# Cosine phases made by an integer addition on Pool instead of an absolute value on ScalarE, and half of the kernel scalings moved from VectorE to ScalarE

## The chip, the cores and the metric

The kernel runs on one core of one Trainium2 chip. Its time is the device time of one execution in microseconds (us). The core has five engines that run side by side: TensorE (PE in the profile, with its weight loads as PEld), VectorE (DVE), ScalarE (ACT), GpSimd or Pool (POOL) and SyncE (SP, which issues most DMAs). Each engine takes its instructions strictly in order and waits on semaphores for the others.

## The reference

The reference is one transformer-like block with two halves; the second half needs the whole output of the first.

```python
h = layernorm(x) * (1 + ca) + sa                  # x: 1 x 2048 x 640
K = einsum("dn,dnl,dn->dl", C, exp(dt*A * l), dt*B).real   # l = 0..2047, N = 128 complex states
y = irfft(rfft(h, 4096) * rfft(K, 4096))[:2048] + h * Dskip   # one convolution for each of 640 channels
x = x + ga * y
h = layernorm(x) * (1 + cb) + sb
x = x + gb * ((silu(h @ w1) * (h @ w3)) @ w2)     # 640 -> 1728 -> 640
```

The six vectors sa, ca, ga, sb, cb, gb come from `silu(c) @ w_mod`. Everything is float32. What matters here is K: for every channel and state a complex power exp(dt*A*l) is wanted at 2048 positions. The kernel writes l = 64a + b and makes small tables of cosine and sine over a (32 slow values) and b (64 fast values, made as two halves), and lets TensorE multiply and sum over the states.

## The kernel before, in words

The 640 channels are cut into 40 table steps of 16 channels. Work on one step s, by the two-letter words that the program uses for it:

- PH (function `phases`, on Pool, for two steps at once): the angle of each of 32 channels and 64 table places as a 32-bit integer, where 2^32 is a full turn and the addition wraps. Three Pool instructions: a product of `thi` and `iota` (128x1376), an addition of `phi` (128x256), an addition of the parts (128x768). They write one of three buffers `ph`.
- AB and CO (`absph`, `cosine`, on ScalarE, two steps at once): the absolute value of the angle into one of two buffers `cs` (128x2048), then in place the sine of a quarter turn less that value, which is the cosine.
- SI (`sine`, ScalarE, in place in `ph`).
- PA, XA, PQ, XQ: exponents on TensorE and exponentials on ScalarE, into a table `A`.
- E1, E2, A1, A2 (`real1` to `imag2`, VectorE, one step each): the tables times the cosine into `E`, and times the sine in place in `A`. E1 and A1 are 128x1024, E2 and A2 128x512. All four read both their inputs from SBUF. The last reader of a `cs` buffer is E2 of the second step of its pair; the last reader of a `ph` buffer is A2 of that step.
- kg (TensorE) sums over the states into the PSUM tile `pk`; K (`k1evac`, VectorE) adds the skip term to 128x4 of it and writes `pk` times the gate `gaT` into `K1` (128x256); pt (TensorE) and uk (a copy on ScalarE) are the first stage of K's transform.

Beside these steps runs the convolution itself, one group of four frequencies at a time: st (TensorE, tile `p`), kc (a ScalarE copy out of `p`), T (two VectorE products that read `p` in PSUM), Y (two VectorE sums that read one input in PSUM), iv (TensorE, `pz`) and zt (ScalarE copy and store).

Steps 0 to 9 or so are made in a front part in which a table of words orders everything, beside the first layer norm. The rest follows the table `ROUND`, four steps in a round; a word `E1+5` in round r means E1 of step 4r+5. It is an order for each engine's queue: nothing is rearranged at run time.

```python
ROUND = (
    "E1+2 pt+0 CO+4 kg+1 A1+2 kc+2 SI+4 T+2 PA+4 uk+0 XA+4 Y+2 E2+2 st+3 K+1 zt+1 kc+3 A2+2 kg+2 "
    "PQ+4 XQ+4 pt+1 E1+3 uk+1 PA+5 PH+6 XA+5 E2+3 K+2 pt+2 A1+3 E1+4 A2+3 T+3 PQ+5 uk+2 Y+3 XQ+5 "
    "iv+2 PA+6 A1+4 kg+3 XA+6 AB+6 PQ+6 XQ+6 st+4 PA+7 K+3 iv+3 kc+4 XA+7 E1+5 PQ+7 zt+3 T+4 LS+4 "
    "Y+4 XQ+7 SI+6 E2+4 LP+4 A2+4 st+5 kc+5 CO+6 E2+5 PH+8 LC+4 A1+5 LO+4 kg+4 A2+5 pt+3 T+5 uk+3 "
    "iv+4 K+4 Y+5 st+6 iv+5 AB+8 "
).split()
```

LS, LP, LC and LO are small pieces for the second half's modulation, in rounds 2 to 6 alone. After the rounds the convolution drains, and from about 375 us on the second half runs, almost all of it matrix products.

Nearly all instructions are issued through one helper, so that the profile shows line 115 for them; they are told apart by engine and tile.

Of the kernel before, what the change touches and what calls it, by code (L numbers as in the profile page):

```python
# [9 lines left out]
F32 = mybir.dt.float32  # L10
F32R = mybir.dt.float32r
I32 = mybir.dt.int32
AF = mybir.ActivationFunctionType
OP = mybir.AluOpType
# [3 lines left out]
P = 128  # L18
# [3 lines left out]
NA, NB = 32, 64  # L22
DC = 128
NDC = D // DC
SD = 16
# [7 lines left out]
NPH = 2 * NA  # L33
NG = NA // 8
NPG = NPH + NG - 1
LATE = 5
IDLE = 16
TURN = 4294967296.0
# [3 lines left out]
def consts():  # L42

    a = np.arange(NA)[:, None]
    f1 = np.arange(NA)[None, :]
    ang = 2 * np.pi * a * (f1 + 0.25) / NA
    s1 = np.zeros((4, NA, 2, 4, NA))
    s1r = np.zeros((4, NA, 2, NA))
    for q in range(4):
        s1[q, :, 0, q, :] = np.cos(ang)  # L50
        s1[q, :, 1, q, :] = -np.sin(ang)
        s1r[q, :, 0] = np.cos(ang)
        s1r[q, :, 1] = -np.sin(ang)
    s1r = s1r.transpose(0, 1, 3, 2).reshape(P, 2 * NA)
    b = np.arange(NB)[:, None, None]
    g1 = np.arange(NA)[None, :, None]
    f2 = np.arange(NB)[None, None, :]
    th = 2 * np.pi * (b * (g1 + 0.25) / L + b * f2 / NB)
    s2 = np.zeros((2, NB, NA, 2, NB))
    s2[0, :, :, 0] = np.cos(th)  # L60
    s2[1, :, :, 0] = np.sin(th)
    s2[0, :, :, 1] = -np.sin(th)
    s2[1, :, :, 1] = np.cos(th)
    s2 = s2.reshape(P, NA, P)

    i1 = (s2.transpose(2, 1, 0) / L).reshape(2, NB, NA // 2, 2, P).transpose(3, 1, 2, 0, 4).reshape(P, NA // 2, 2, P)
    i1 = i1.reshape(P, NA // 2, 2, 2, 4, 4, 4).transpose(0, 1, 2, 5, 4, 6, 3).reshape(P, NA // 2, 2, P)
    i2 = np.concatenate([np.cos(ang).T, -np.sin(ang).T] * 2)
    f_late = np.arange(4 * LATE, NA)
    i2late = np.stack([i2[f_late], i2[NA + f_late]])  # L70
    i2b = np.einsum("lm,cfa->lcfma", np.eye(4), i2late).reshape(8, 8 - LATE, 4 * P)

    slow = np.roll(np.arange(NA), -8)
    s1 = s1[:, slow].reshape(P, 2, P)

    iota = np.concatenate([-(128 * slow[-8:] + 63), 2 * np.arange(NA) + 1, -1024 * np.arange(1, NG)])
    iota = np.tile(iota.astype(np.int32), (P, 1))

    row = np.arange(P)
    selx = row[:, None] % 8 == np.arange(8)  # L80
    of_m = row[:, None] // 8 % 2 == 1
    stepx = np.where(of_m, np.repeat((0, 0.5), (NB, NA)), np.concatenate([np.arange(NB), 64.0 * slow]))
    is_lo = (row // 16 % 2)[:, None]

    c1 = s1r.reshape(4, NA, 2 * NA).sum(axis=1, keepdims=True).repeat(NA, axis=1).reshape(P, 2 * NA)

    one4 = (np.arange(P) % NA == 0).astype(np.float32)[:, None]

    toq = np.arange(P)[:, None] % 4 == np.arange(P)[None] // NA
    tog = np.arange(P)[:, None] // 4 == np.arange(NA)[None]  # L90
    c1c = np.tile(c1[0], 2)[:, None]
    misc = np.concatenate([selx, stepx, s1r, c1, one4, toq, tog, is_lo, 1 - 2 * is_lo, c1c], axis=1)
    f = lambda v: np.ascontiguousarray(v, dtype=np.float32)
    return {"s1": f(s1), "s2": f(s2), "i1": f(i1), "i2": f(i2), "i2b": f(i2b), "iota": iota, "misc": f(misc),
            "ident": np.eye(P, dtype=np.float32)}


def bc(ap, axis, n):
    v = ap.unsqueeze(axis)
    shape = list(v.shape)  # L100
    shape[axis] = n
    return v.broadcast_to(shape)
# [18 lines left out]
def tile_kernel(ctx: ExitStack, tc: tile.TileContext, a):  # L121
    nc = tc.nc
    V, S, G, PE = nc.vector, nc.scalar, nc.gpsimd, nc.tensor
# [19 lines left out]
    V, S, G, PE, Q = (InOrder(tc, e, (front,)) for e in (nc.vector, nc.scalar, nc.gpsimd, nc.tensor, nc.sync))  # L143

    def keep(ins):

        return tc.keep_in_program_order(ins) if in_order[0] else ins

    def act(*args, **kw):

        return tc.keep_in_program_order(S.activation(*args, **kw))
# [18 lines left out]
    ssm = ExitStack()  # L170
    kp = ssm.enter_context(tc.tile_pool(name="kp", bufs=1, side="right"))
    s1 = kp.tile([P, 2, P], F32, name="s1")
    iota = kp.tile([P, NPG - NA + 8], I32, name="iota")
    gaT = kp.tile([P, D // 4], F32, name="gaT")
    dz = kp.tile([P, D // 4], F32, name="dz")
    V.memset(dz, 0.0)
# [6 lines left out]
    def phase_tile():  # L183
        return php.tile([P, 2 * SD, NPG], I32, name="ph")
# [5 lines left out]
    tp = tabs.enter_context(tc.tile_pool(name="tp", bufs=2, reuse_waits="tile"))  # L190
    once = lambda shape, dt, name: tp.tile(shape, dt, name=name, bufs=1)
    thi = once([P, D], I32, "thi")
# [360 lines left out]
    ph, cs, AA, EC, PK, K1 = {}, {}, {}, {}, {}, {}  # L553
# [40 lines left out]
    def phases(s):  # L594
        sl = slice(s * SD, s * SD + 2 * SD)
        p = phase_tile()
        hold = tc.keep_in_program_order if 0 < s < 4 else keep
        b0 = NA - 8
        base = p[:, :, b0:NA]
        hold(G.tensor_tensor(p[:, :, b0:], bc(thi[:, sl], 2, NPG - b0), bc(iota, 1, 2 * SD), op=OP.mult))  # L600
        keep(G.tensor_tensor(base, base, bc(phi[:, sl], 2, 8), op=OP.add))
        keep(G.tensor_tensor(p[:, :, :b0].rearrange("p k (g j) -> p k g j", j=8), bc(base, 2, NG - 1),
                             bc(p[:, :, NPH:], 3, 8), op=OP.add))
        ph[s] = p[:, :, :NPH]

    def absph(s):
        cs[s] = tp.tile([P, 2 * SD, NPH], F32, name="cs")
        act(cs[s], ph[s], AF.Abs)

    def cosine(s):  # L610
        c = cs.pop(s)
        act(c, c, AF.Sin, scale=-2 * math.pi / TURN, bias=math.pi / 2)
        cs[s], cs[s + 1] = c[:, :SD], c[:, SD:]

    def sine(s):
# [5 lines left out]
    def trig(s):  # L621
        cosine(s)
        sine(s)
# [33 lines left out]
    def k1evac(s):  # L657
        dst = tp.tile([P, SD // 4, NB], F32, name="K1")
        pk = PK.pop(s)
        keep(V.tensor_tensor(pk[:, :, 0], pk[:, :, 0], dz[:, s * 4:s * 4 + 4], op=OP.add))  # L660
        keep(V.tensor_tensor(dst, pk, bc(gaT[:, s * 4:s * 4 + 4], 2, NB), op=OP.mult))
        K1[s] = dst

    PT = {}
# [243 lines left out]
    def conv_part(fn):  # L908
        return lambda k: fn((k - LAG) // 8, (k - LAG) % 8)

    parts = {"PH": phases, "AB": absph, "CO": cosine, "SI": sine, "PA": lambda k: exp_fast((k,)), "XA": fast,
             "PQ": lambda k: exp_slow((k,)), "XQ": slow, "E1": real1, "E2": real2, "A1": imag1, "A2": imag2,
             "kg": kgen, "K": k1evac, "pt": k_stage1, "uk": k_out}
    conv = {"st": conv_part(stage2), "kc": conv_part(k_copy), "T": conv_part(products), "Y": conv_part(sums),
            "iv": conv_part(inverse1), "zt": conv_part(z_store)}
# [86 lines left out]
    for word in FRONT:  # L1002
        name, k = word[:2].rstrip("+"), int(word[len(word[:2].rstrip("+")):])
# [25 lines left out]
    for rnd in range(NS // EB):  # L1029
        if 2 <= rnd < 7:  # L1030
            late_load(rnd - 2)
        for word in ROUND:
            name, k = word[:2].rstrip("+-"), EB * rnd + int(word[len(word[:2].rstrip("+-")):])
# [16 lines left out]
    for tk in range(NS + 1, LAG + 8 * NDC + 2):  # L1050
# [17 lines left out]
        i = tk - 1 - LAG - 8 * NDC + 8  # L1068
# [40 lines left out]
    V, S, G, PE = (InOrder(tc, e, (in_order,)) for e in (nc.vector, nc.scalar, nc.gpsimd, nc.tensor))  # L1109
# [521 lines left out]
def arrange(inputs):  # L1631
    global _CONST
    if _CONST is None:
        _CONST = consts()
    A = np.ascontiguousarray
    g = {k: np.asarray(v) for k, v in inputs.items()}
    x = g["A_u"].reshape(NA, NB, D).transpose(1, 0, 2).reshape(L, D)
    w1, w3 = g["B_w1"], g["B_w3"]
    nf = NFT - 1

    def ftile(w):
        n = w.shape[1] // P
        return w.reshape(KD, P, n, P).transpose(2, 1, 0, 3)

    mixed = np.concatenate([w1[:, nf * P:], w3[:, nf * P:]], axis=1)
    r = {
        "x": A(x),
        "prm": A(np.stack([g[k].T for k in ("A_A_re", "A_A_im", "A_B_re", "A_B_im", "A_C_re", "A_C_im")])),
        "log_dt": A(g["A_log_dt"].reshape(1, D)),
        "D": A(g["A_Dskip"].reshape(1, D)),  # L1650
        "c": A(g["c"].reshape(KD, P).T),
        "w_mod": A(g["w_mod"].reshape(KD, P, 8, 480).transpose(2, 1, 0, 3)),
        "wg": A(np.concatenate([ftile(w1[:, :nf * P]), ftile(mixed)])),
        "wu": A(ftile(w3[:, :nf * P])),
        "w2": A(g["B_w2"]),
    }
    r.update(_CONST)
    return r
# [17 lines left out]
```

## Time and profile before

| | |
|---|---|
| median of 3 runs | 929.85 us (928.87 to 930.47) |
| the profiled execution's own time | 937.06 us |
| span of its trace | 935.1 us |
| busy share of the span | PE 93%, DVE 75%, ACT 58%, POOL 29% |
| the chain that ended last | PE 73%, DVE 9%, ACT 8%, DMA 5% |

The shares are means over stages that differ: the front part (to about 125 us), the rounds (to about 310 us), the drain, and the second half. Rows of the timeline view read: start, duration, engine, line, operation, output<-inputs with partitions x elements, count of merged instructions, and in brackets the idle time of the engine just before and what ended it. Durations of neighbours on VectorE and ScalarE overlap by about 0.1 us (the end of one is still being written when the next begins), so an instruction's share of its engine is the distance to the next start.

### The profile page before, as it was taken

How to read it: one execution, taken by the hardware profiler on the slowest of the kernel's cores; microseconds unless marked ns; L12 is line 12 of the kernel's file. 1: busy time of each engine (PE TensorE's matmuls, PEld its weight loads, DVE VectorE, ACT ScalarE, POOL GpSimd, SP SyncE). 2: the span in 40 equal slices, each digit the busy share in tenths (PEclk: the TensorE clock that was granted, in tenths of full speed). 3: DMA queues.
4: the chain of work that ended last, by engine and by line, in shares of the span. 5: the costliest groups of instructions: out<-in, count | busy, mean ns of one | idle time of the engine just before them, and what ended most of it. 6: DMA issues, size and time to landing. Idle time of an engine off the chain costs nothing.

```text
span 935.1 us, 20139 instructions
## 1 busy us (share of the span) xinstructions
PE 873.9 (93%) x8082; PEld 668.0 (71%) x8082; DVE 700.7 (75%) x1209; ACT 542.0 (58%) x747; POOL 273.8 (29%) x285
## 2 busy tenths in 40 slices
PE   3898879999998899999999999899999999999997
PEld 2545456666666576688888887678888888888886
DVE  5899889999999968677666666577976666654674
ACT  6989889999999632574333333475634333323332
POOL 3333435543544222304222203210332222100341
PEclk9967789999999999999999999999999999999999
DMA  8664375766666967943222239846321312123352
GB/s 264 218 215 172 149 212 169 223 176 190 177 214 183 297 211 223 299 136 99 56 57 57 57 105 242 231 127 197 99 62 52 113 57 57 57 87 97 102 196 82
DMA packets 103328, 140.68 MB, mean 150 GB/s; under 512 B 19940, under 2 KB 62436, under 8 KB 103236
## 3 DMA queue, kind: packets, MB, share of 16 engines
q1 hardware_dynamic: 92532, 113.71, 40.8%
q10 hardware_dynamic: 8272, 18.16, 6.6%
q0 software_dynamic: 2432, 7.54, 2.6%
q8 instruction: 63, 1.03, 0.5%
q14 instruction: 29, 0.24, 0.1%
HBM read 107.92 MB, written 31.46 MB: 149 GB/s over the span
## 4 chain that ended last, share of the span: by engine, by line
PE 73%; DVE 9%; ACT 8%; DMA 5%; issue 3%; POOL 0%; SPq 0%; DVEq 0%; ACTq 0%; POOLq 0%
PE ps L115 54%; PE p L115 6%; PE pz L115 3%; PE pt L115 2%; PE pk L115 2%; DMA rw<-in_w_dram 2%; PE pa L115 2%; PE pu L115 2%; ACT A L115 1%; DVE A L115 1%; DVE uk L115 1%; DVE E L115 1%; ACT cs L115 1%; DVE u L115 1%; ACT uk L115 1%
## 5 line engine op out<-in xcount | busy, mean ns | idle before, releaser
L115 DVE TENSOR_TENSOR s<-ps,s 128x512 f32<-128x512 f32 x138 | 94.8, 687 | 82.6 <-PE ps L115 82.3
L115 ACT CAST gh<-rw 128x640 fp32r<-128x640 f32 x87 | 63.3, 727 | 119.6 <-PE ps L115 90.6
L115 DVE TENSOR_TENSOR gl<-rw,gh 128x640 fp32r<-128x640 f32 x87 | 78.3, 900 | 64.4 <-ACT gh L115 64.4
L115 POOL TENSOR_TENSOR S<-rw 128x256 f32<-128x256 f32 x46 | 36.5, 795 | 233.5 <-DVE S0l L115 155.5
L115 PE MATMUL ps<-xA,gh 128*128 128x512 f32 x280 | 88.0, 392 | 0.6 <-ACT xA L115 0.6
L115 PE MATMUL ps<-gh,uh 128*128 128x512 f32 x224 | 87.7, 392 | 0.0
L115 PE MATMUL ps<-gl,uh 128*128 128x512 f32 x224 | 87.3, 390 | 0.0
L115 POOL TENSOR_TENSOR ph<-thi,iota 128x1376 int32<-128x1376 int32 x20 | 51.2, 2562 | 118.4 <-DVE A L115 103.5
L115 PE MATMUL p<-uk,s 128*64 128x256 f32 x576 | 71.6, 391 | 15.2 <-issue 3.8
L115 DVE TENSOR_TENSOR E<-A,cs 128x1024 f32<-128x1024 f32 (+1 forms) x80 | 80.8, 1021 | 1.6 <-PE pk L115 1.4
L115 PE MATMUL ps<-gh,ul 128*128 128x512 f32 x208 | 81.1, 390 | 0.0
L115 ACT ACTIVATE A<-pa 128x1024 f32<-128x1024 f32 (+1 forms) x80 | 64.3, 815 | 9.9 <-PE pa L115 9.6
L115 PEld LDWEIGHTS p<-uk,s 128*64 128x64 f32 x576 | 41.3, 138 | 36.8 <-DVE Y L115 5.6
L115 PEld LDWEIGHTS ps<-xA,gh 128*128 128x128 f32 x280 | 52.3, 188 | 13.6 <-ACT xA L115 1.2
L115 DVE TENSOR_TENSOR A<-A,ph 128x1024 f32<-128x1024 f32 x40 | 54.1, 1356 | 0.8
L115 PE MATMUL ps<-xA,gl 128*128 128x512 f32 x140 | 54.5, 390 | 0.0
L115 PE MATMUL pt<-s,K 128*64 128x128 f32 x640 | 45.1, 285 | 6.1 <-ACT uk L115 5.9
L115 PEld LDWEIGHTS ps<-gh,uh 128*128 128x128 f32 x224 | 42.2, 188 | 9.4 <-DVE h L115 0.6
L115 ACT ACTIVATE s<-ps 128x512 f32<-128x512 f32 (+1 forms) x33 | 19.7, 597 | 50.0 <-PE ps L115 50.0
L115 PEld LDWEIGHTS ps<-gl,uh 128*128 128x128 f32 x224 | 42.2, 188 | 8.9
L115 PEld LDWEIGHTS pt<-s,K 128*64 128x64 f32 x640 | 35.7, 140 | 14.4 <-ACT uk L115 9.7
L115 POOL TENSOR_TENSOR rw<-rw,gbr 128x512 f32<-128x512 f32 x14 | 20.3, 1453 | 86.6 <-DMA rw<-in_w_dram 84.6
(224 smaller groups left out, 2227.9 us busy)
## 6 DMA issues: line engine op xcount, KB each, us to landing
rw<-in_w_dram ACTq DMA_DIRECT2D x44, 320.0 KB, 3.1
us<-u SPq DMA_DIRECT2D x16, 640.0 KB, 3.5
rw<-in_wg_dram SPq DMA_DIRECT2D x31, 320.0 KB, 2.9
s<-in_s_dram SPq DMA_DIRECT2D x36, 256.0 KB, 4.0
i<-in_i_dram SPq DMA_DIRECT2D x36, 256.0 KB, 4.2
rw<-in_wu_dram SPq DMA_DIRECT2D x28, 320.0 KB, 3.0
uk<-us SPq DMA_DIRECT2D x16, 512.0 KB, 5.9
zs<-zt SPq DMA_DIRECT2D x16, 512.0 KB, 4.3
```

Of the source, the lines that this page charges most:

```text
L115: ins = fn(*args, **kw)
```

## The change

For steps 12 to 39 the cosine is now the sine of the angle plus a quarter turn. The addition is an integer one on Pool (a constant 2^30 from one more column of `iota`, wrapping), from `ph` into `cs`; ScalarE's absolute value is gone there, and the sine takes integers as it did in SI. Besides, for even steps from 12 on, the scaling of `pk` by the gate is made by ScalarE in four 128x64 instructions, each with its gate column as the scale, and no more by VectorE in one 128x256 instruction.

```diff
-    iota = np.concatenate([-(128 * slow[-8:] + 63), 2 * np.arange(NA) + 1, -1024 * np.arange(1, NG)])
+    iota = np.concatenate([-(128 * slow[-8:] + 63), 2 * np.arange(NA) + 1, -1024 * np.arange(1, NG), [1 << 30]])
...
+    quarter = iota[:, NPG - NA + 8:]
...
     def absph(s):
-        cs[s] = tp.tile([P, 2 * SD, NPH], F32, name="cs")
-        act(cs[s], ph[s], AF.Abs)
+        c = tp.tile([P, 2 * SD, NPH], F32, name="cs")
+        if s < 12:
+            act(c, ph[s], AF.Abs)
+            cs[s] = c
+        else:
+            cs[s] = c.bitcast(I32)
+            keep(G.tensor_tensor(cs[s], ph[s], bc(quarter.broadcast_to([P, NPH]), 1, 2 * SD), op=OP.add))
 
     def cosine(s):
         c = cs.pop(s)
-        act(c, c, AF.Sin, scale=-2 * math.pi / TURN, bias=math.pi / 2)
+        if s < 12:
+            act(c, c, AF.Sin, scale=-2 * math.pi / TURN, bias=math.pi / 2)
+        else:
+            i, c = c, c.bitcast(F32)
+            act(c, i, AF.Sin, scale=2 * math.pi / TURN)
         cs[s], cs[s + 1] = c[:, :SD], c[:, SD:]
...
         keep(V.tensor_tensor(pk[:, :, 0], pk[:, :, 0], dz[:, s * 4:s * 4 + 4], op=OP.add))
-        keep(V.tensor_tensor(dst, pk, bc(gaT[:, s * 4:s * 4 + 4], 2, NB), op=OP.mult))
+        if s < 12 or s % 2:
+            keep(V.tensor_tensor(dst, pk, bc(gaT[:, s * 4:s * 4 + 4], 2, NB), op=OP.mult))
+        else:
+            for g in range(SD // 4):
+                act(dst[:, g], pk[:, g], AF.Identity, scale=gaT[:, s * 4 + g:s * 4 + g + 1])
```

Where the instructions stand now is seen on two engines. First Pool's queue in the rounds, before; the numbers behind names tell buffers apart, and each three rows are one PH:

```order
L115 TENSOR_TENSOR ph_1894<-thi_95,iota_75 128x32x43 [waits DVE_49,Activation_49]
L115 TENSOR_TENSOR ph_1894<-ph_1894,phi_96 128x32x8 [waits Pool_49]
L115 TENSOR_TENSOR ph_1894<-ph_1894 128x32x24 [waits Pool_49]
L115 TENSOR_TENSOR ph_2057<-thi_95,iota_75 128x32x43 [waits DVE_49,Activation_49]
L115 TENSOR_TENSOR ph_2057<-ph_2057,phi_96 128x32x8 [waits Pool_49]
L115 TENSOR_TENSOR ph_2057<-ph_2057 128x32x24 [waits Pool_49]
```

So far Pool did nothing here but one PH after the other. The same place of Pool's queue now:

```order
L115 TENSOR_TENSOR cs_1984<-ph_1897,iota_75 128x2048 [waits DVE_49,Activation_49,Pool_49]
L115 TENSOR_TENSOR ph_2063<-thi_95,iota_75 128x32x43 [waits DVE_49]
L115 TENSOR_TENSOR ph_2063<-ph_2063,phi_96 128x32x8 [waits Pool_49]
L115 TENSOR_TENSOR ph_2063<-ph_2063 128x32x24 [waits Pool_49]
L115 TENSOR_TENSOR cs_2160<-ph_2063,iota_75 128x2048 [waits DVE_49,Activation_49,Pool_49]
```

One 128x2048 addition now stands between any two PH, and each waits for VectorE, whose E2 frees the `cs` buffer that is to be written.

Second, VectorE's queue in the middle of a round (E1 and E2 of step 15, K, A1 of step 15, E1 of step 16), before:

```order
L115 TENSOR_TENSOR E_1888<-A_1617,cs_1584 128x16x64
L115 TENSOR_TENSOR E_1888<-A_1617,cs_1584 128x16x32
L115 TENSOR_TENSOR pk_1842<-pk_1842,dz_77 128x4 [waits DVE_49,PE_49]
L115 TENSOR_TENSOR K1_1901<-pk_1842,gaT_76 128x256 [waits DVE_49]
L115 TENSOR_TENSOR A_1617<-A_1617,ph_1502 128x16x64
L115 TENSOR_TENSOR E_1914<-A_1815,cs_1755 128x16x64 [waits Activation_49]
```

The fourth row is the scaling of an even step's `pk`. The same place now:

```order
L115 TENSOR_TENSOR E_1891<-A_1617,cs_1584 128x16x64
L115 TENSOR_TENSOR E_1891<-A_1617,cs_1584 128x16x32
L115 TENSOR_TENSOR pk_1845<-pk_1845,dz_77 128x4 [waits DVE_49,PE_49]
L115 TENSOR_TENSOR A_1617<-A_1617,ph_1502 128x16x64 [waits DVE_49]
L115 TENSOR_TENSOR E_1920<-A_1818,cs_1758 128x16x64 [waits Activation_49]
L115 SCALAR_TENSOR_TENSOR A_1617<-ph_1502,A_1617 128x16x32 [waits DVE_49]
```

The row that wrote `K1` is gone from here; the rest keeps its order. The second row (E2) is the one for which Pool's addition into `cs_1984` waits.

More of the change, by code (lines that the diff above doesn't have):

```diff
@@ L172, in tile_kernel @@
     s1 = kp.tile([P, 2, P], F32, name="s1")
-    iota = kp.tile([P, NPG - NA + 8], I32, name="iota")
+    iota = kp.tile([P, NPG - NA + 9], I32, name="iota")
+    quarter = iota[:, NPG - NA + 8:]
     gaT = kp.tile([P, D // 4], F32, name="gaT")
@@ L599, in phases @@
         base = p[:, :, b0:NA]
-        hold(G.tensor_tensor(p[:, :, b0:], bc(thi[:, sl], 2, NPG - b0), bc(iota, 1, 2 * SD), op=OP.mult))
+        hold(G.tensor_tensor(p[:, :, b0:], bc(thi[:, sl], 2, NPG - b0), bc(iota[:, :NPG - b0], 1, 2 * SD), op=OP.mult))
         keep(G.tensor_tensor(base, base, bc(phi[:, sl], 2, 8), op=OP.add))
```

## The prediction

> **What bounds the kernel now.** The change touches only the rounds, so I read the table of busy times by stretch first, cut at E1+2 (the first VectorE word of a round). Columns: stretch, its length, then busy time of PE, PEld, DVE, ACT, POOL, granted clock, DMA share.
>
> ```profile
> core 0: us, PE busy (x) PEld busy (x) DVE busy (x) ACT busy (x) POOL busy (x), PEclk, DMA share, GB/s
> 208.06:235.48 27.42, 25.50 (x480) 17.92 (x480) 25.84 (x44) 25.97 (x27) 13.02 (x7) 1.00 0.68 197
> sum 135.42, PE 125.25 PEld 89.62 DVE 127.90 ACT 128.14 POOL 65.39; mean PE 25.05 PEld 17.92 DVE 25.58 ACT 25.63 POOL 13.08
> ```
>
> The sum is over five rounds: 135.42 / 5 = 27.08 us a round, in which PE, DVE and ACT are each busy for 25 to 26 us and POOL for 13. Three engines are balanced, and POOL looks half empty. Busy times don't say whose work has slack, so the timeline of VectorE in one round is next. The names of the words stand in the text behind it.
>
> ```profile
> 208.06 1.29 DVE L115 TENSOR_TENSOR E<-A,cs 128x1024 f32<-128x1024 f32 x1
> ...
> 212.03 0.69 DVE L115 TENSOR_TENSOR T<-p,kc 128x512 f32<-128x512 f32 x1 [1.10 <-ACT kc L115]
> ...
> 215.90 1.82 DVE L115 TENSOR_TENSOR E<-A,cs 128x1024 f32<-128x1024 f32 x2
> 217.63 0.16 DVE L115 TENSOR_TENSOR pk<-pk,dz 128x4 f32<-128x4 f32 x1
> 217.83 0.42 DVE L115 TENSOR_TENSOR K<-pk,gaT 128x256 f32<-128x256 f32 x1
> 218.17 1.22 DVE L115 TENSOR_TENSOR A<-A,ph 128x1024 f32<-128x1024 f32 x1
> 219.30 1.22 DVE L115 TENSOR_TENSOR E<-A,cs 128x1024 f32<-128x1024 f32 x1
> 220.44 0.69 DVE L115 SCALAR_TENSOR_TENSOR A<-ph,A 128x512 f32<-128x512 f32 x1
> 221.04 0.68 DVE L115 TENSOR_TENSOR T<-p,kc 128x512 f32<-128x512 f32 x1
> ...
> 223.16 1.69 DVE L115 TENSOR_TENSOR A<-A,ph 128x1024 f32<-128x1024 f32 x1
> ...
> 230.23 0.68 DVE L115 TENSOR_TENSOR E<-A,cs 128x512 f32<-128x512 f32 x1
> 230.83 1.22 DVE L115 TENSOR_TENSOR A<-A,ph 128x1024 f32<-128x1024 f32 x1
> 231.97 0.15 DVE L115 COPY modT<-pm 128x1 f32<-128x1 f32 x1
> ...
> 232.36 0.68 DVE L115 SCALAR_TENSOR_TENSOR A<-ph,A 128x512 f32<-128x512 f32 x1
> ```
>
> VectorE runs without a gap except for T+2 (212.03), which waits 1.10 us for ScalarE's kc. So VectorE sets the round, with ScalarE close behind. One row is too long: A1+4 at 223.16 takes 1.69 us, its like at 218.17 takes 1.22. Pool's timeline tells why.
>
> ```profile
> 221.26 2.50 POOL L115 TENSOR_TENSOR ph<-thi,iota 128x1376 int32<-128x1376 int32 x1 [8.87 <-DVE A L115]
> 223.85 1.50 POOL L115 TENSOR_TENSOR ph<-ph,phi 128x256 int32<-128x256 int32 x1
> ...
> 233.19 2.51 POOL L115 TENSOR_TENSOR ph<-thi,iota 128x1376 int32<-128x1376 int32 x1 [5.21 <-DVE A L115]
> ```
>
> Pool's product ends at 223.76. If A1+4 could not start before that, it ends near 223.76 + 1.1 = 224.86; the row ends at 224.85. (The small addition behind it, at 223.85, is long in its turn; more on it below.) Two collisions from the front part, a DVE and a POOL row each, show the same more grossly:
>
> ```profile
> 26.82 2.51 POOL L115 TENSOR_TENSOR ph<-thi,iota 128x1376 int32<-128x1376 int32 x1
> 27.21 3.19 DVE L115 TENSOR_TENSOR E<-A,cs 128x1024 f32<-128x1024 f32 x1 [0.21 <-ACT cs L115]
> ...
> 97.49 1.22 DVE L115 TENSOR_TENSOR E<-A,cs 128x1024 f32<-128x1024 f32 x1
> 97.71 3.35 POOL L115 TENSOR_TENSOR ph<-thi,iota 128x1376 int32<-128x1376 int32 x1 [4.61 <-DVE A L115]
> ```
>
> At 27.21 Pool is first: E takes 3.19 us and ends at 30.40, which is Pool's end (29.33) plus 1.07. At 97.71 VectorE is first: Pool takes 3.35 us instead of 2.50 and ends at 101.06, that is 98.56 plus 2.50. **Pool's arithmetic and the E and A words, both inputs of which lie in SBUF, exclude each other for whole instructions; who comes first runs through.** The T at 221.04, which reads PSUM, keeps its 0.68 us beside Pool's product: VectorE's work on PSUM is the only cover that Pool's work has. On this the prediction rests.
>
> **What the new addition costs on Pool.** No row shows 128x2048. Smallest, median and largest duration in ns of the forms that exist:
>
> ```profile
> L115 POOL TENSOR_TENSOR ph<-thi,iota x20: 2497/2505/3354, 15.3 to 286.6; 128x1376 int32<-128x1376 int32 x20
> L115 POOL TENSOR_TENSOR ph<-ph,phi x20: 640/1501/1662, 17.9 to 289.2; 128x256 int32<-128x256 int32 x20
> L115 POOL TENSOR_TENSOR ph<-ph x20: 1580/2460/2634, 18.6 to 289.9; 128x768 int32<-128x768 int32 x20
> L115 POOL TENSOR_TENSOR S<-rw x46: 727/742/1658, 424.8 to 807.7; 128x256 f32<-128x256 f32 x46
> L115 POOL TENSOR_TENSOR rw<-rw,gbr x14: 1288/1401/1879, 870.6 to 914.7; 128x512 f32<-128x512 f32 x14
> ```
>
> The second row fits the exclusion: 0.64 us at the least, but 1.50 at 223.85, where A1+4 ran until 224.85 (224.85 + 0.64 = 225.49; the row ends at 225.35).
>
> The last two forms read two full tensors: (1288 - 742) / 256 = 2.13 ns an element and 0.19 us fixed, so 0.19 + 2048 x 2.13 ns = 4.6 us, the upper bound. The phase forms repeat an operand as the new one does (its constant): the product gives (2500 - 190) / 1376 = 1.68 ns, so 3.6 us, the lower bound; the 768 addition gives 1.82 ns, so 3.9 us. I take 3.8, between the two int32 forms.
>
> "GPSIMD Engine Reference" of the Trainium skill, section 3.1, gives 4497 ns for an addition of two float tensors of 2048 elements a partition; the f32 rows above agree with it, the int32 rows lie below. By 4.5 us for each of 14 additions the sum below would be an estimated 10 us larger.
>
> **The fourteen additions on the path.** AB+6 of a round (steps 14, 18, ... 38: seven) waits for E2+3, the second of the two at 215.90, which ends at 217.72; Pool starts some 0.13 us after a release (A2 at 220.44 ends at 221.13, Pool's product starts at 221.26). From there to T+3 at 221.04 VectorE has nothing but A1+3, E1+4 and A2+3, all on SBUF, after 0.2 us of pk. Whether Pool gets in before A1+3 or after it, the next of the three stands still for the addition: 3.8 us, less some 0.05. 7 x 3.75 = 26.3 us.
>
> AB+8 (steps 12, 16, ... 36: seven) waits for E2+5, which ends at 230.91. A1+5 follows without a gap and goes first; Pool has its turn at about 231.9, until 235.7. Only the two small copies between 231.97 and 232.36 run beside it; A2+5, due at 232.36, stands until 235.7: 3.34 us. So in the five rounds with these copies; without them 3.73. The first one, step 12, falls into the end of the front part:
>
> ```profile
> 122.40 1.28 DVE L115 SCALAR_TENSOR_TENSOR A<-ph,A 128x512 f32<-128x512 f32 x2
> 124.92 0.17 DVE L115 TENSOR_TENSOR pk<-pk,dz 128x4 f32<-128x4 f32 x1 [1.24 <-PE pk L115]
> ```
>
> There an idle stretch of 1.24 us follows, so it costs 2.5. Sum: 2.5 + 5 x 3.34 + 3.73 = 22.9. Both together **+49.2 us**.
>
> Queued on Pool behind the additions is the next PH. It is released by A2, which the stall itself delays, so it keeps its place relative to VectorE, and its old collisions (0.5 us at 223.16) stay and are in the 27.08.
>
> **What is saved.** ScalarE loses an Abs twice a round, and gains eight small scalings:
>
> ```profile
> 234.72 1.93 ACT L115 ACTIVATE cs<-ph 128x2048 f32<-128x2048 int32 x1
> 236.69 1.91 ACT L115 ACTIVATE cs<-cs 128x2048 f32<-128x2048 f32 x1
> 238.51 0.57 ACT L115 COPY kc<-p 128x512 f32<-128x512 f32 x1
> ```
>
> Two rows of the view by groups, with the sum and the mean in ns behind the first bar and the waits behind the second (of the front part, and of the five rounds):
>
> ```profile
> L115 ACT ACTIVATE uk<-uk,tiny 128x128 f32<-128x128 f32 x1 | 0.4, 388 | 0.0
> L115 DVE TENSOR_TENSOR T<-p,kc 128x512 f32<-128x512 f32 x20 | 13.7, 685 | 5.1 <-ACT kc L115 5.1
> ```
>
> A form with an operand column takes 388 ns at 128 elements. With (1930 - 388) / 1920 = 0.8 ns an element that is 0.34 us at 64, and 0.25 from start to start, since neighbours overlap by 0.09 (236.69 + 1.91 against 238.51): four are 1.0 us. ScalarE saves 2 x 1.9 - 2 x 1.0 = 1.8 us a round, but it is off the path by then, so only its waits count: T waited 5.1 us for kc in five rounds. In the new order, counted from the start of A2+5: T, p and pk end at 2.1, ScalarE's scaling at 3.2, CO at 5.0, kc at 5.6; VectorE reaches T+2 at 6.1: Pool's product, released at 0.7, holds E1+2 until 3.3, then come E1+2 (1.1), Pool's small addition (0.64) and A1+2 (1.1). The wait should go: -5 us (0 to -6). The K that leaves VectorE saves 218.17 - 217.83 = 0.34 us at K+2, seven times, -2.4. At K+0 it saves nothing: E1+2 waits there for Pool's product anyway (the 1.29 at 208.06). PE, at 25.05 us a round, is no bound for a round of 33.
>
> Sum: 49.2 - 5 - 2.4 = **+41.8 us**, six a round: the profiled execution would go from 937.06 (span 935.1) to 979. The median of the runs shown is 929.85, 7.2 below the profiled one; I add the same difference and predict **971 us**. With 3.6 us an addition and all waits gone it is +38, with 4.6 and no wait gone +57. So this case spans 968 to 987.
>
> **Rivals.** *Hidden, and faster.* Pool idles 14 us a round (27.08 - 13.08); were its additions to run beside VectorE, there would remain 14 x 0.34 = 4.8 us of K and 5 of kc: 920 us. For it: Pool is on no long stretch of the path. Against it: the stretch behind E2+3 holds no PSUM work, and no row shows an E or A word at its normal length while Pool's arithmetic advances. It decides if the exclusion does not hold for this form of addition. "Perfetto Trace Analysis" of the Trainium skill, section Optimizing Scalar/DVE Operations, says that with VectorE saturated offloading "to Scalar (or even GPSIMD) may make sense", and warns of the shared SBUF port in the next sentence; the first half is this rival, and the rows at 27.21 and 97.71 bear out the second. *Half exposed.* The addition shares the way into SBUF more finely than the product does, or finds PSUM work beside it in one of its two places: about 20 us slower, 950. *Nothing visible.* PE and ScalarE, at 25 and 26 of 27 us, set the round and take up VectorE's stalls. But VectorE's own idle time is 1 us a round, so 7 us of stall don't fit; it needs an addition of 0.9 us (2 x 0.9 is the 1.0 of kc, 0.34 of K and 0.4 of the copies): 930.
>
> **Chances.** Exposed 0.83, half 0.06, hidden 0.07, nothing visible 0.04. Within 0.2% (about 1.9 us, what a measurement of this kernel tells from no change) is the last; faster 0.07; slower 0.89. The range leaves out the hidden and the unchanged case and part of the half exposed one below, and a little above 986: 957 to 986.
>
> **What would show it.** In the new profile: a Pool row cs<-ph,iota of 3.6 to 4.6 us, fourteen times; VectorE rows E<-A,cs or A<-A,ph of about 5 us at AB+6 and A<-ph,A of about 4 us at AB+8; rounds of 33 us; T's wait for kc near zero; ScalarE idle 8 us a round. Wrong if rounds stay at 27 us, or if the addition's row is under 2 us. If the rows are long but the round is not, another engine set it.

## The result and the profile after

| | before | changed |
|---|---|---|
| median | 929.37 us (928.87 to 930.47) | 978.50 us (975.89 to 981.17) |
| the profiled execution's own time | 937.06 us | 981.17 us |
| span of its trace | 935.1 us | 978.9 us |

The changed kernel is slower: the ratio is 1.0515 (95% interval 1.0491 to 1.0538), 49.1 us by the medians. 971 was predicted, with a range of 957 to 986.

The same five rounds of both kernels are compared below, cut at the words T (from the 5th T to the 25th). The rows are of the view by stretch: stretch, length, busy time of PE, PEld, DVE, ACT and POOL, granted clock, DMA share, GB/s. Before:

```profile
157.86:293.37 135.51, 125.30 (x2392) 89.82 (x2388) 129.13 (x212) 128.23 (x131) 64.55 (x31) 1.00 0.64 189
```

The changed kernel:

```profile
165.50:336.18 170.68, 142.42 (x2392) 99.59 (x2390) 158.68 (x202) 119.92 (x161) 105.52 (x41) 0.88 0.50 150
```

Five rounds grew by 35.2 us. VectorE is busy for 29.6 of these (158.68 - 129.13), although it has ten instructions fewer, and idle for 5.6 more (12.0 against 6.4). The granted clock fell from 1.00 to 0.88, which nothing in the prediction had foreseen. The groups of VectorE in these stretches (sum and mean in ns behind the first bar, idle time before them behind the second) say which instructions grew. Before:

```profile
L115 DVE TENSOR_TENSOR A<-A,ph 128x1024 f32<-128x1024 f32 x20 | 28.9, 1447 | 0.5
L115 DVE TENSOR_TENSOR E<-A,cs 128x1024 f32<-128x1024 f32 x20 | 25.0, 1251 | 0.0
L115 DVE SCALAR_TENSOR_TENSOR A<-ph,A 128x512 f32<-128x512 f32 x20 | 13.6, 681 | 0.0
L115 DVE TENSOR_TENSOR K<-pk,gaT 128x256 f32<-128x256 f32 x20 | 8.5, 424 | 0.7
L115 DVE TENSOR_TENSOR pk<-pk,dz 128x4 f32<-128x4 f32 x20 | 3.2, 159 | 0.0
L115 DVE TENSOR_SCALAR modT<-modT 128x5 f32<-128x5 f32 x1 | 0.2, 155 | 0.0
```

The changed kernel:

```profile
L115 DVE TENSOR_TENSOR A<-A,ph 128x1024 f32<-128x1024 f32 x20 | 43.8, 2188 | 0.9 <-DVE E L115 0.5
L115 DVE SCALAR_TENSOR_TENSOR A<-ph,A 128x512 f32<-128x512 f32 x20 | 26.8, 1342 | 0.0
L115 DVE TENSOR_TENSOR E<-A,cs 128x1024 f32<-128x1024 f32 x20 | 26.7, 1333 | 0.0
L115 DVE TENSOR_TENSOR T<-p,kc 128x512 f32<-128x512 f32 x21 | 14.4, 684 | 6.5 <-ACT kc L115 6.4
L115 DVE TENSOR_TENSOR K<-pk,gaT 128x256 f32<-128x256 f32 x10 | 4.2, 424 | 0.3
L115 DVE TENSOR_TENSOR pk<-pk,dz 128x4 f32<-128x4 f32 x20 | 3.3, 164 | 3.2 <-PE pk L115 3.2
L115 DVE TENSOR_SCALAR modT<-modT 128x5 f32<-128x5 f32 x1 | 3.2, 3198 | 0.0
```

A1 (A<-A,ph) grew by 14.9 us. Five of its words stand beside the addition at AB+6 and take 4.42 to 4.65 us in place of 1.22, which makes 16.3; the collisions of A1 with PH lost 1.4. A2 (A<-ph,A) grew by 13.2 and a tiny tensor_scalar by 3.0: 16.2 together, which is the addition at AB+8, five times 3.0 to 3.4. E grew by 1.7. K lost 4.3. Of the idle time, T's wait for kc did not go: 6.4 us after, 5.1 before. A new wait of 3.2 us for pk stands beside it.

The timeline of the changed kernel shows one stall of each kind and the tensor_scalar. Columns: start, duration, engine, line, operation, output<-inputs, and in brackets the idle time ahead of it.

```profile
240.78 3.63 POOL L115 TENSOR_TENSOR cs<-ph,iota 128x2048 int32<-128x2048 int32 x1 [6.17 <-DVE E L115]
241.06 4.43 DVE L115 TENSOR_TENSOR A<-A,ph 128x1024 f32<-128x1024 f32 x1
...
258.67 4.45 POOL L115 TENSOR_TENSOR cs<-ph,iota 128x2048 int32<-128x2048 int32 x1 [4.65 <-DVE E L115]
259.94 3.72 DVE L115 SCALAR_TENSOR_TENSOR A<-ph,A 128x512 f32<-128x512 f32 x1
...
292.42 4.45 POOL L115 TENSOR_TENSOR cs<-ph,iota 128x2048 int32<-128x2048 int32 x1 [3.11 <-DVE E L115]
293.70 3.20 DVE L115 TENSOR_SCALAR modT<-modT 128x5 f32<-128x5 f32 x1
```

At 241.06 Pool is 0.28 us ahead, and A1 takes 4.43 us in place of 1.22: it ends 1.08 behind Pool's end at 244.41. At 258.67 Pool waits for A1 (4.45 in place of 3.62), and then A2, due at 259.94, stands until Pool ends at 263.12 and takes 0.54 more. The tensor_scalar at 293.70, which reads and writes five elements a partition, stands in the same way. The same view behind another stall at AB+8:

```profile
229.36 0.93 ACT L115 ACTIVATE K<-pk,gaT 128x64 f32<-128x64 f32 x4 [2.79 <-DVE pk L115]
230.04 3.68 PE L115 MATMUL p<-uk,s 128*64 128x256 f32 x16 [3.62 <-DVE Y L115]
233.82 0.58 ACT L115 COPY kc<-p 128x512 f32<-128x512 f32 x1 [1.74 <-PE p L115]
234.44 0.69 DVE L115 TENSOR_TENSOR T<-p,kc 128x512 f32<-128x512 f32 x1 [1.27 <-ACT kc L115]
```

This is the surprise. While A2 stands, and until Y follows it, TensorE is out of work for 3.62 us. Its next p then takes 3.68 us. ScalarE's kc waits for p, and T for kc. The same word of a round before:

```profile
235.66 1.95 PE L115 MATMUL p<-uk,s 128*64 128x256 f32 x16 [0.89 <-ACT uk L115]
```

### The profile page after: what moved, and what is told of

Its sections match the earlier page's. It is cut to its first block, busy times and chain, and to the rows that moved or that the text cites. A ratio compares the mean times of both kernels' runs of the same rounds, so it can differ in the third digit from the quotient of the medians.

```text
span 978.9 us, 20209 instructions
## 1 busy us (share of the span) xinstructions
PE 896.6 (92%) x8082; PEld 682.1 (70%) x8082; DVE 741.2 (76%) x1195; ACT 530.1 (54%) x789; POOL 330.3 (34%) x299
## 4 chain that ended last, share of the span: by engine, by line
PE 75%; DVE 16%; DMA 4%; ACT 3%; issue 2%; SPq 0%; POOL 0%; DVEq 0%; ACTq 0%; POOLq 0%
PE ps L115 54%; PE p L115 7%; DVE A L115 6%; PE pk L115 3%; PE pz L115 3%; PE pu L115 2%; PE pt L115 2%; DVE E L115 2%; DVE p L115 1%; PE pa L115 1%; DVE T L115 1%; DMA s<-in_s_dram 1%; DVE Y L115 1%; DVE uk L115 1%; DVE u L115 1%
## 5 line engine op out<-in xcount | busy, mean ns | idle before, releaser
L115 PE MATMUL p<-uk,s 128*64 128x256 f32 x576 | 82.8, 437 | 32.5 <-DVE Y L115 12.6
L115 PEld LDWEIGHTS p<-uk,s 128*64 128x64 f32 x576 | 44.3, 153 | 59.4 <-issue 17.6
L115 DVE TENSOR_TENSOR E<-A,cs 128x1024 f32<-128x1024 f32 (+1 forms) x80 | 83.5, 1055 | 2.6 <-PE pk L115 1.9
L115 POOL TENSOR_TENSOR cs<-ph,iota 128x2048 int32<-128x2048 int32 x14 | 56.0, 4001 | 58.8 <-DVE E L115 54.5
L115 DVE TENSOR_TENSOR A<-A,ph 128x1024 f32<-128x1024 f32 x40 | 73.9, 1852 | 1.2 <-DVE E L115 0.5
L115 PE MATMUL pt<-s,K 128*64 128x128 f32 x640 | 47.6, 294 | 12.6 <-ACT K L115 9.2
L115 PEld LDWEIGHTS pt<-s,K 128*64 128x64 f32 x640 | 37.7, 147 | 22.6 <-ACT K L115 11.6
L115 PEld LDWEIGHTS pz<-Y,i 64*128 64x128 f32 x576 | 40.8, 215 | 11.0 <-issue 9.5
```

What stands on the lines that cost most here:

```text
L115: ins = fn(*args, **kw)
```

## The experiments

Times are medians; ratios are to the kernel before, run on the same chip (929.3 to 932.0 us there). In the table the five rounds are those of the view by stretch above, with VectorE's share.

| kernel | median, us | ratio (95%) | five rounds | DVE busy | DVE idle |
|---|---|---|---|---|---|
| before | 929.4 | | 135.5 | 129.1 | 6.4 |
| the change | 978.5 | 1.0515 (1.0491 to 1.0538) | 170.7 | 158.7 | 12.0 |
| cosine alone | 978.3 | 1.0520 (1.0493 to 1.0546) | 170.3 | 158.6 | 11.7 |
| K alone | 947.6 | 1.0208 (1.0171 to 1.0246) | 150.3 | 132.2 | 18.2 |
| before, with a zero added | 964.9 | 1.0383 (1.0359 to 1.0407) | 159.4 | 151.2 | 8.2 |
| before, with memsets | 938.2 | 1.0095 (1.0068 to 1.0123) | 139.3 | 136.8 | 2.5 |
| addition in four pieces | 966.5 | 1.0398 (1.0360 to 1.0435) | 160.1 | 154.1 | 6.0 |
| addition at AB+8 alone | 963.5 | 1.0348 (1.0314 to 1.0382) | 158.4 | 145.3 | 13.1 |
| addition at AB+6 alone | 961.7 | 1.0339 (1.0312 to 1.0365) | 159.9 | 145.6 | 14.4 |
| the change, TensorE kept busy, 48 | 982.6 | 1.0546 (1.0505 to 1.0587) | 172.2 | 159.4 | 12.8 |
| the change, TensorE kept busy, 28 | 970.4 | 1.0401 (1.0362 to 1.0440) | 162.1 | 158.4 | 3.6 |

The theory to begin with was the prediction's: Pool's reading and VectorE's words on two SBUF tiles exclude each other. Its rivals were that the move of K to ScalarE costs the time, or the new order of waits (E2, then Pool, then ScalarE), not the exclusion.

### The two halves of the change

The cosine alone: every K back on VectorE, the rest as in the change.

```
-        if s < 12 or s % 2:
-            keep(V.tensor_tensor(dst, pk, bc(gaT...), op=OP.mult))
-        else:
-            for g in range(SD // 4):
-                act(dst[:, g], pk[:, g], AF.Identity, scale=gaT...)
+        keep(V.tensor_tensor(dst, pk, bc(gaT...), op=OP.mult))
```

> The change's cosine part alone: Pool's addition for steps 12 to 39 as in the change, all K scalings back on VectorE. Theory A (exclusion: VectorE's words with two SBUF inputs stand still while Pool adds): the 14 stalls of some 3.7 us stay, VectorE gets 7 x 0.34 us back and TensorE no longer waits for ScalarE's K, so 974 to 984 us. Theory B (the cost lies in K's move to ScalarE, whose in-order queue now holds TensorE: the profile of the change shows TensorE waiting some 15 us for ScalarE's K in five rounds): at most 945 us.

978.25 us: the cosine is the whole loss, and K's move is worth nothing within the change. The five rounds show why: VectorE's K words come back, yet its busy time is the same (158.6) and the round too. K reads PSUM, so it runs beside Pool's work, and the word behind it stands that much less:

```profile
204.27 3.63 POOL L115 TENSOR_TENSOR cs<-ph,iota 128x2048 int32<-128x2048 int32 x1 [5.78 <-DVE E L115]
...
204.68 0.42 DVE L115 TENSOR_TENSOR K<-pk,gaT 128x256 f32<-128x256 f32 x1
205.02 3.96 DVE L115 TENSOR_TENSOR A<-A,ph 128x1024 f32<-128x1024 f32 x1
```

A1 at AB+6 takes 3.96 to 4.14 us here and 4.42 to 4.65 in the change. In five rounds A1 is 2.0 us shorter and E another 2.0, beside the 4.3 of K.

K alone: the kernel before with the reverse of that edit (even K from step 12 on by ScalarE, the absolute value kept).

> The change's K part alone: even K from step 12 on scaled by ScalarE, the absolute value stays on ScalarE for all steps. Theory A: no exclusion is added; ScalarE's 25.6 us a round grow by 2.0 to 27.6 and pass VectorE, so 0.5 to 1.5 us a round for seven rounds, 933 to 942 us, rounds of 27.6 to 28.6. Theory B: most of the 49 us is here, 960 to 975 us.

947.59 us, between the two forecasts. K's move, worth nothing within the change, costs 18 us alone. The stretch of five rounds:

```profile
156.11:306.44 150.33, 130.22 (x2393) 92.00 (x2389) 132.16 (x201) 136.76 (x171) 60.46 (x30) 0.97 0.55 170
```

From the list of its waits over the same rounds (us in total, times, longest):

```profile
DVE T L115 <- ACT kc L115: 9.4, 7, 2.0
...
PE pt L115 <- ACT K L115: 6.9, 5, 1.4
```

ScalarE's 136.8 us of work are more than the 135.5 that five rounds took before, so it is the bound without any wait. That is 1.3 of the 14.8 us by which five rounds grew. VectorE's idle time grew by 11.8 and its busy time by 3.0, although K left it: E<-A,cs 128x1024, which meets Pool's product, takes 32.1 us where it took 25.0. The waits on ScalarE's in-order queue, of T for kc and of TensorE for K, are seen here, but their shares stay open. In the change the Abs are gone (119.9 us busy) and there is room for K. So the halves don't add: 18 and 49 make 49.

### Pool's reading, or the new waits

Before, with a zero added: Pool adds a column of zeros to `ph` in place, behind each PH from step 12 on; the Abs stays on ScalarE.

```
         ph[s] = p[:, :, :NPH]
+        if s >= 12:
+            keep(G.tensor_tensor(ph[s], ph[s], bc(none.broadcast_to([P, NPH]), 1, 2 * SD), op=OP.add))
```

> The kernel before with one more Pool instruction behind each PH from step 12 on: zero is added in place to the 128x2048 angles. ScalarE's absolute value, VectorE and TensorE keep all their work, and Pool has idle time there (the angles are read 11 and 7 us after they are made), so nothing is made late by it. Theory A: the additions of 3.6 us meet VectorE's E and A words: behind PH+6 some 1.8 us are covered by T, p and Y and 1.8 to 2 exposed, behind PH+8 some 0.6 covered and 3 exposed; 5 us a round less up to 1 of kc, so 957 to 968 us; E and A rows of 3 to 5 us. Theory C (the change is slow because its cosine comes late or because the queues behind it wait): 929 to 932 us.

964.85 us, as the exclusion has it: 35.6 us for an instruction of the same shape that leaves every value as it was. The timeline shows a word that did not stand in the change, E2, standing here:

```profile
214.24 3.62 POOL L115 TENSOR_TENSOR ph<-ph,iota 128x2048 int32<-128x2048 int32 x1
...
214.75 3.66 DVE L115 TENSOR_TENSOR E<-A,cs 128x512 f32<-128x512 f32 x1
```

E2 normally takes 0.68 us. It ends 0.55 us behind Pool's 217.86.

Before, with memsets: Pool fills the `cs` tile twice ahead of each Abs from step 12 on. That keeps the change's chain of waits (VectorE's E2 frees `cs`, Pool writes it for 3.67 us, ScalarE waits for Pool), but Pool reads nothing.

```
         cs[s] = tp.tile([P, 2 * SD, NPH], F32, name="cs")
+        if s >= 12:
+            for _ in range(2):
+                keep(G.memset(cs[s], 0.0))
         act(cs[s], ph[s], AF.Abs)
```

> The kernel before with two Pool memsets of the 128x2048 cs tile ahead of each absolute value from step 12 on (the absolute value overwrites them). They wait for the same E2 as the change's additions and take about as long (some 2 us each), and ScalarE waits for them, but they read nothing. Theory A, by which Pool's reads of SBUF are what excludes: no E or A word becomes longer, the absolute value of AB+8 is some 0.6 us late, 930 to 937 us. If any work of Pool excludes VectorE, or if the wait E2 - Pool - ScalarE is what costs (theory C): 960 to 980 us.

938.15 us: 8.9 us, a little above the forecast and far from the 49. Both places in the timeline:

```profile
221.70 3.67 POOL L115 MEMSET cs<- 128x2048 f32 x2 [4.26 <-DVE pk L115]
222.04 1.21 DVE L115 TENSOR_TENSOR A<-A,ph 128x1024 f32<-128x1024 f32 x1
223.17 1.22 DVE L115 TENSOR_TENSOR E<-A,cs 128x1024 f32<-128x1024 f32 x1
224.31 0.69 DVE L115 SCALAR_TENSOR_TENSOR A<-ph,A 128x512 f32<-128x512 f32 x1
...
235.11 3.67 POOL L115 MEMSET cs<- 128x2048 f32 x2 [3.06 <-DVE E L115]
...
236.44 0.69 DVE L115 SCALAR_TENSOR_TENSOR A<-ph,A 128x512 f32<-128x512 f32 x1
```

Beside 3.67 us of Pool's writing A1, E1 and A2 keep their length. PH, which starts behind the memsets, now meets E1+2: in five rounds E1 takes 32.9 us in place of 25.0. T's wait for kc (5.1) went in return, so these rounds grew by 3.8; the rest of the 8.9 us lies outside of them and was not taken apart. One word does stand beside the writing, the tensor_scalar on 128x5: 0.50 us in place of 0.155, until the first of two memsets ends. So what costs the words with two SBUF inputs is Pool's addition, which reads SBUF, neither that Pool is busy nor that ScalarE waits for it. A memset also computes nothing, so these two runs do not part reading from computing. "SBUF — State Buffer" of the Trainium skill, section Who interferes with whom, lays it on the reading: a VectorE instruction with two SBUF inputs contends with a GpSimd instruction that reads SBUF, "not with one that only writes it". These two runs agree.

### How long the exclusion lasts, and what two places cost

In four pieces: the change, with each addition issued as four of 128x512.

```
-            keep(G.tensor_tensor(cs[s], ph[s], bc(quarter...), op=OP.add))
+            for i in range(0, 2 * SD, 8):
+                keep(G.tensor_tensor(cs[s][:, i:i + 8], ph[s][:, i:i + 8], bc(quarter...), op=OP.add))
```

> The change, with each addition of 128x2048 issued as four of 128x512. Theory A (VectorE is held for the time of Pool's instruction, however it is cut; a piece should take about 3.62/4 = 0.91 us): a VectorE word between two SBUF tiles waits for one piece at a time and the pieces wait for it, so the words beside an addition grow by 0.9 us each instead of one by 3 us, the sum of the stalls stays, and the time is 970 to 985 us. Rival C (what costs is the length of one Pool instruction, and short ones slip into VectorE's gaps between words): 935 to 960 us. Rival D (a Pool instruction has a fixed cost that makes four much longer than one): over 990 us, with pieces of clearly more than 0.91 us.

966.46 us, below the first forecast and above the second. The pieces by their tile, with the smallest, median and largest duration in ns:

```profile
L115 POOL TENSOR_TENSOR cs<-ph,iota x56: 1032/1488/2026, 121.5 to 333.9; 128x512 int32<-128x512 int32 x56
```

In the timeline the pieces and VectorE take turns:

```profile
233.24 6.45 POOL L115 TENSOR_TENSOR cs<-ph,iota 128x512 int32<-128x512 int32 x4 [3.60 <-DVE E L115]
234.14 1.22 DVE L115 TENSOR_TENSOR A<-A,ph 128x1024 f32<-128x1024 f32 x1
235.28 2.06 DVE L115 TENSOR_TENSOR E<-A,cs 128x1024 f32<-128x1024 f32 x1
237.27 1.52 DVE L115 SCALAR_TENSOR_TENSOR A<-ph,A 128x512 f32<-128x512 f32 x1
```

Each word waits for one piece (E1 0.84 us, A2 0.84), and the four pieces need 6.45 us, since they wait for the words. So an instruction holds the way for its own length, and shorter ones share it. VectorE's stalls shrink (154.1 busy for 158.7) and its idle time halves, which is the larger part of the gain; the last two experiments tell why.

One place at a time, every K on VectorE: the addition only at AB+8, or only at AB+6, the other place with the Abs. The edit, in `absph` and `cosine`, is this condition for AB+8, and `!= 2` for AB+6:

```
-        if s < 12:
+        if s < 12 or s % 4 != 0:
```

> Every K on VectorE, and the addition only in the round's last place (AB+8, table steps 12, 16, ... 36, seven times); the other seven keep the absolute value. Theory A (each place has its own price, as the sum of the prediction has it: 22.9 us here): 947 to 957 us, up to 3 us each for the wait of T after it. Rival C (the two places share one price, since the first stall of a round already gives the others time): 965 us or more here or with the other place alone. Rival D (only the other place costs): 928 to 935 us.

> Every K on VectorE, and the addition only in the place in the middle of the round (AB+6, table steps 14, 18, ... 38, seven times). Theory A (26.3 us by the sum of the prediction): 950 to 960 us, and with the other place alone the two differences add to 45 to 53 us, the change's own. Rival C (one shared price): 965 us or more. Rival D: 928 to 935 us.

963.49 and 961.74 us, both above the sum's forecasts: 32 us each by the ratios (0.0348 and 0.0339 of 930), 64 together where both at once cost 48. The stalls do add up, nearly: VectorE's busy time grows by 16.2 and 16.4, and by 29.5 with both. Its idle time doesn't: it grows by 6.7 and 8.0, and by 5.3 with both. So the price of a place is 16 us of stall in five rounds, as in the prediction's kind of sum, plus waits for TensorE and ScalarE that do not add.

### TensorE's clock

What those waits are, the timeline of the changed kernel had suggested: a TensorE that idled for 3.6 us resumes slowly. To test it, matmuls of the constants `s1` with themselves, which nobody reads, are issued into TensorE's gap in seven rounds of the changed kernel: behind iv+4, ahead of st+6.

```
+            if word == "iv+4" and 1 <= rnd < 8:
+                wake = psS.tile([P, 4, P], F32, name="wake", tag="pb", bufs=1)
+                for i in range(48):
+                    r = i % 2 * 64
+                    keep(PE.matmul(wake[r:r + 64, i // 2 % 4, :], s1[:, 0, :64], s1[:, 1, :], ...))
```

> The change, with 48 matmuls of the constants s1 with themselves (nobody reads them) issued on TensorE in each of the seven rounds, behind iv+4 and ahead of st+6, where TensorE sits idle for 3.6 us while VectorE is held; by the row of pt (16 in 1.09 us) they take 3.3 us. Theory A (TensorE's idle time lowers its granted clock, which makes the matmul p after it 3.7 us instead of 1.95, kc late, and keeps T+2's wait of 1.2 to 1.5 us): p takes 1.95 us in that place, T's wait for kc there goes, and the time falls by 6 to 12 us, to 966 to 972. Rival C (p is long for another cause, such as operands that are late): p stays at 3.7 us and the time is 975 to 985. Rival D (the fillers push st+6 back): p at 1.95 us but later, time 980 or more.

982.58 us: p took 1.90 us, but started 2 us late, so the third theory (the filling pushes st+6 back) is what came. The filling was mis-sized: the 48 matmuls take 5.46 us, since each counts as two in the row of pt from which I had reckoned 3.3. What T's wait costs can't be told from that, so the same with `range(28)`:

> The change with 28 of the filling matmuls in place of 48. The 48 took 5.46 us by the profile, 2 us more than TensorE's gap, so st+6 started 2 us late, though its p then took 1.90 us; 28 take 3.2 us and end before VectorE's Y+5 releases st+6. Theory A (the lower clock after the gap is what keeps T+2's wait for kc): p takes 1.9 us at the place where it took 3.7, T's wait there falls from 1.2 to 1.5 us to near zero, and the time falls by 6 to 12 us against the change, to 966 to 972. Rival C (kc is late for another cause): p takes 1.9 us and the time is 975 to 985.

970.39 us. One of these rounds:

```profile
191.72 3.28 PE L115 MATMUL wake<-s 128*64 128x128 f32 x56 [0.19 <-ACT uk L115]
...
195.15 1.95 PE L115 MATMUL p<-uk,s 128*64 128x256 f32 x16 [0.16 <-DVE Y L115]
...
197.20 0.58 ACT L115 COPY kc<-p 128x512 f32<-128x512 f32 x1
198.21 0.68 DVE L115 TENSOR_TENSOR T<-p,kc 128x512 f32<-128x512 f32 x1
```

p is back at 1.95 us, kc is done 0.43 us before T starts, and T waits no more. The stretch of five rounds:

```profile
164.76:326.83 162.07, 145.78 (x2668) 105.98 (x2668) 158.43 (x202) 119.28 (x161) 110.15 (x41) 0.97 0.51 158
```

VectorE is busy for as long as in the change (158.4 against 158.7), and 8.4 of the 8.6 us come off its idle time (12.0 to 3.6). Work that computes nothing made the changed kernel faster by 8.1 us by the medians, and by 10.6 by the ratios, each to the runs of before beside it. The clock is at 0.97 instead of 0.88.

The gap of 3.6 us is not the only place where the clock fell. Cut at two falls in one round of the changed kernel, the view by stretch gives: stretch, length, PE's busy time, granted clock, DMA share, GB/s.

```profile
224.93:228.34 3.41, 1.49 (x24) 1.00 1.11 266
228.34:235.17 6.83, 5.13 (x30) 0.50 0.41 116
242.00:245.41 3.41, 2.02 (x27) 1.00 1.13 329
245.41:252.24 6.83, 6.83 (x94) 0.50 0.16 49
```

At 228.34 the clock halved within the gap, and at 245.41 while TensorE worked, after 1.39 us without work ahead of pt. Here too p is long, and T waits:

```profile
250.51 2.78 PE L115 MATMUL p<-uk,s 128*64 128x256 f32 x16
...
254.01 0.69 DVE L115 TENSOR_TENSOR T<-p,kc 128x512 f32<-128x512 f32 x1 [1.45 <-ACT kc L115]
```

In the five rounds the clock was at half for 39.0 us in the change and for 10.2 with the 28 matmuls. Of the five gaps of 1.4 us ahead of pt in the change, three were followed by the low clock and two were not; what decides it stays open. "TensorE: Matmul & The Clock Gate" of the Trainium skill, Part 1, says that TensorE falls to half its clock after an idle window of about 3.4 us, and is back after as long a busy one. The half clock is in these rows, and it lasted for 6.83 us, twice 3.41. That a whole window must be idle is not: 1.92 and 1.39 us of the 3.41 before were enough, and the measurement decides.

### The kernel before, profiled again

The first profiled execution of before, from which all durations of the prediction come, was 7 us above its median. So the same kernel was profiled once more.

> The kernel before, unchanged, profiled a second time, since its first profiled execution (937.06 us) is 7 us above its median. Theory A (that profile lost its 7 us outside of the rounds): 928 to 931 us with rounds of 27.1 us, 232 to 234 us between the first T and the last one, and about 568 us from the last T to the end of the span, where the first profile has 573. Rival C (the rounds differ): the stretch from the first T to the last differs by 5 us or more.

931.36 us, span 929.3. The timelines give:

| profiled execution | first T | last T | between | from the last T to the end |
|---|---|---|---|---|
| before | 129.2 | 362.0 | 232.8 | 573.1 |
| before, again | 126.9 | 359.7 | 232.8 | 569.6 |
| the change | 132.9 | 409.7 | 276.8 | 569.2 |

Its row of five rounds:

```profile
155.58:291.11 135.53, 125.30 (x2393) 89.81 (x2388) 129.20 (x212) 128.26 (x131) 64.50 (x31) 1.00 0.62 189
```

The rounds are the same to 0.1 us; the first profile lost its time ahead of the first T (2.3) and behind the last (3.5). So 44.0 us of the change lie between the first and the last T, and the rest ahead of the first: 3.7 to 6.0 us. The word that meets the addition of step 12 (the A2 pair at 122.40 in the first profile of before) starts 10.0 us ahead of the first T in the change, and 6.8 and 6.5 us ahead of it in the two profiles of before, so this addition costs about 3.2 to 3.4. What is ahead of that word differs between executions of the same code: it starts at 122.94 in the change, and at 121.19 and 120.46 in the two kernels with filling matmuls, whose first ones come later.

## Why the prediction was right, and where its terms were off

Right, and shown by the runs: the exclusion, its consequence that the additions lie on VectorE's path whole, and the side (1.0515). The zero added and the memsets single out Pool's addition, which reads SBUF, as against its being busy or the new waits; no run left room for the hidden, the half exposed or the unchanged case. The rows forecast are there: fourteen additions of 3.62 to 4.46 us, A2 near 4 us, rounds of 32 to 36 us, a ScalarE with 10 us of slack a round (170.7 - 119.9 over five). A1 at AB+6 took 4.4 to 4.7 instead of about 5.

The sum was +41.8 us, and the medians differ by 49.1. The mechanism held. Of the three terms the additions were off in size, and the two savings did not come:

- **The additions, +49.2.** Taken at 3.8 us each on Pool; they take 3.62, the lower bound of the estimate, where they don't wait themselves. A stall was 3.2 to 3.4 us at AB+6 and 3.0 to 3.4 at AB+8, not 3.75 and 3.34: at AB+6 Pool also has a start of up to 0.28 us, not 0.05 (240.78 against 241.06). In five rounds 32.5 us (16.3 + 16.2) where the sum has 35.5. Step 12 cost 3.2 to 3.4 where the sum has 2.5.
- **T's wait for kc, -5.** This term was wrong outright: the wait is 6.4 us in five rounds after 5.1 before. The working gave kc at 5.6 us and VectorE at T+2 at 6.1, and that order would have held, had p taken its 1.95 us. I had written "PE, at 25.05 us a round, is no bound for a round of 33", and had asked only whether TensorE has time, not what the stall's idle time does to its speed. With TensorE kept busy the wait falls to 1.2 us, and the kernel to 970.4; its five rounds grew by 26.6 us (162.1 - 135.5), where the sum has 28.8.
- **K, -2.4.** K left VectorE with 4.3 us in five rounds, but the cosine alone takes the same time as the change, so none of it reached the end. The working had counted K+2 as saved whole, 1.7 us in five rounds, though K reads PSUM and so is just the cover for Pool that the working names: without it A1 stands 2.0 us longer. And what K alone costs (18 us) the prediction did not ask.

New, and in no term: 3.2 us of waits for pk in five rounds, which go too when TensorE is kept busy. In five rounds the prediction has 35.5 - 5 - 1.7 = 28.8 us; measured 35.2. The errors have both signs: the stalls were taken 3.0 us too large, and the 6.7 of savings did not come. That the time came as near to 971 as it did is in part luck.

The step from the profiled to the median time (7.2 us) held: what the first profile of before had lost against the second lay outside of the rounds.

## What to carry to other kernels

Ask of work that moves to Pool whether it reads SBUF and which VectorE instructions beside it have two SBUF operands, not how idle Pool is: an addition of 3.6 us held VectorE for 3.0 to 3.4 us, and writing of the same length held none of its words with two SBUF inputs. A word that reads PSUM is cover for Pool's work, so moving it away from VectorE can save nothing. A stall on one engine is also idle time on the others, and on TensorE that idle time can be paid a second time, as a halved clock, so a gap that a change opens on TensorE belongs in its sum. Parts of a change that share slack don't add: 18 and 49 us made 49, and 32 and 32 made 48.

## What the runs showed of the hardware that was not expected

- After an idle stretch of 3.6 us TensorE took 3.68 us for p where it had taken 1.95. The clock also halved after a gap of 1.39 us, for 6.83 us, and p took 2.78 there. Filling the longer gap with matmuls that nobody reads gained 8.1 us.
- A tensor_scalar on 128x5 elements with one SBUF input, normally 0.155 us, took 3.20 us beside Pool's addition (the row at 293.70), and so stood like the words with two inputs; beside a memset it took 0.50. The T and p words, which read PSUM, kept 0.69 and 0.70 us beside Pool's addition of zeros (at 197.13 and 197.86 in that run).
- Pool's memset of 128x2048 takes 1.81 us (3.67 for two) and holds up none of VectorE's words with two SBUF inputs; its integer addition of that size takes 3.62 and holds those that it meets.
